# One relu and one low-part step per PSUM bank in a two-layer feed-forward network

## Chip, cores and metric

One of the eight cores of a Trainium2 chip runs the whole program. The metric is the device time of one execution in microseconds (us); it is given as the median of several runs. Beside it stands one profiled execution, from which all rows come.

## What is computed

Attention with a window of 64 over q, k and v of 8 batches, 8 heads, 576 positions and 64 features, then a Fourier mix of the 8 x 576 x 512 result, a normalisation, and a feed-forward network with two weight matrices (512 x 2048 and 2048 x 512):

```python
scores = scale * np.matmul(q, k.transpose(0, 1, 3, 2))        # masked to a window of 64
attn = softmax(scores)                                        # exp, divided by its sum
x = (attn @ v) as (B, S, H * D)
u = x + real(fft(fft(x, axis=1), axis=2))
un = (u - mean(u)) / sqrt(var(u) + 1e-6)
out = u + np.maximum(un @ w_ch1, 0.0) @ w_ch2
```

The change touches the last line alone: the relu between the two matrix products.

## The kernel before

The 4608 positions are 36 tiles of 128. Attention is done tile by tile (`attn_tile`), the Fourier mix batch by batch (`fft`), the normalisation tile by tile (`norm_tile`), and the feed-forward network for two tiles at a time: 18 chunks of 256 positions (`ffn`, names `c` and `NCH`). Each number is kept as a float16 high part and a float16 low part, and a product is three passes (`PASSES`: high-high, high-low, low-high). Chunk 0 alone is done in float32 (`plain`), while the weights are still converted and split.

In a chunk the 2048 hidden features are 16 blocks of 128, numbered by `f`. For each block:

- the first layer (`one`, L1204) is 12 matmuls of 256 columns into half a PSUM bank. A bank holds the blocks f and f + 1 for an even f, as the tile `ph`; there are two such banks (ring `f1`);
- ScalarE takes the relu of the block's 256 columns into the high part of a tile `hh` (L1219, in chunk 0 L1216);
- VectorE forms the low part, relu minus high part, from the same 256 columns (L1222);
- the second layer (`second`, L1185) is 6 matmuls of 512 columns, which add the block to the two banks `po` of the chunk (ring `f2`, two banks).

The ring `hh` has 4 tiles, so the relu of a block waits until the second layer has used the tile of four blocks earlier. At a chunk's end VectorE adds `po` to the tile `xu` (`last`, L1242, in chunk 0 L1240) and the sum is sent out.

No engine's order is written by hand. The kernel first records every operation with an engine, an estimated duration and a priority (`op`), and `Plan.order` plays them through: at each step it takes the operation that can start earliest, with the priority deciding ties and short waits. The relu and the low part have the priority -10, ahead of nearly all else on their engines; first and second layer have priorities above one million, so that PE (TensorE) does attention and Fourier work when that is ready and fills up with the feed-forward network. Some operations may be given to one of two engines (`alt`). A ring in the list of the planner's constructor hands out its buffers in a fixed order. What the planner's order leaves to wait for is made into semaphore waits afterwards, tile by tile, from what each instruction writes and reads: each engine then works its list strictly in order, and an instruction that waits holds up all behind it.

Of the kernel before, what the change touches and what calls it, by code (L numbers as in the profile page):

```python
# [12 lines left out]
F32 = mybir.dt.float32  # L13
F16 = mybir.dt.float16
# [13 lines left out]
P = 128  # L28
# [7 lines left out]
CH = 256  # L36
NCH = NTT // 2
NKF = DFF // P
XR = 10
TURN = 1.5  # L40
Y_SOON = (4, 8)
LAZY, LAZY_FFT, LAZY_U = 0.2, 0.8, 0.5
# [257 lines left out]
def attn_fft_ffn_kernel(ctx: ExitStack, tc: tile.TileContext, q, k, v, w1, w2, gidx, dft_d, dft_s, mask, out):  # L300
# [8 lines left out]

    RINGS = {  # L310
        "kq": 2, "pr": 2, "pt": 2, "xu": XR, "y": 1, "yT": 1, "tail": 1,
        "xe": 1, "r3": 3, "fh": 5, "g": 2, "mp": 2, "mt": 1, "un": 2, "up": 1, "big": 4, "hh": 4,
        "ps": 4, "f1": 2, "f2": 2,
    }
    plan = Plan(RINGS, ("kq", "pr", "pt", "xu", "y", "yT", "tail", "xe", "r3", "fh", "g", "mp", "f1", "f2", "hh"))
# [5 lines left out]
    def bank(tag, name, shape=(P, 4, P)):  # L321
        return ps.tile(list(shape), F32, tag=tag, name=name, bufs=RINGS[tag])
# [846 lines left out]
    def ffn(c):  # L1169
        plain = c < PLAIN  # L1170
        t = {}
        bpo = [Buf("f2"), Buf("f2")]
        prev = None
        at = 0 if not plain else 1

        def second(f, bh):
            def go():
                if f == 0:
                    t["po"] = [bank("f2", f"po{c}_{i}", (P, DM)) for i in range(2)]
                hh = t["hh", f]  # L1180
                for i in range(2):
                    sl = slice(P * i, P * i + P)
                    mm = [(hh[:, sl], wf[1][f])] if plain else [(hh[:, a, sl], wp[1][:, f, b_]) for a, b_ in PASSES]
                    for x, (l_, r_) in enumerate(mm):
                        nc.tensor.matmul(  # L1185
                            t["po"][i], l_, r_, start=(f == 0 and x == 0), stop=(f == NKF - 1 and x == len(mm) - 1)
                        )

            op("PE", 1.73 if plain else 1.3, 1e6 + 32 * c + 2 * max(f, 1) + 5, go, [bh, Bw[1][f + at]], bpo)

        for f in range(NKF):
            bph, bh = Buf(), Buf("hh")
            if f % 2 == 0:
                bpair, bfirst = Buf("f1"), Buf()
            g0, c0 = 4 * (f // 4), (f % 4) * P

            def one(f=f, g0=g0, c0=c0):
                ph, u = t["ph", f], uhls[c]
                if plain:
                    mm = [(wf[0][g0 + kc][:, c0 : c0 + P], u[:, kc]) for kc in range(4)]  # L1200
                else:
                    mm = [(wp[0][:, g0 + kc, a, c0 : c0 + P], u[:, b_, kc]) for kc in range(4) for a, b_ in PASSES]
                for x, (l_, r_) in enumerate(mm):
                    nc.tensor.matmul(ph, l_, r_, start=(x == 0), stop=(x == len(mm) - 1))  # L1204

            def bank1(f=f, one=one):
                if f % 2 == 0:
                    t["ph2", f] = bank("f1", f"ph{c}_{f}", (P, 2, CH))
                t["ph", f] = t["ph2", f - f % 2][:, f % 2]
                one()  # L1210

            def h_part(z, f=f):
                ph = t["ph", f]
                if plain:
                    t["hh", f] = sb([P, CH], F32, "hh", f"hh{c}_{f}")
                    nc.scalar.activation(t["hh", f], ph, AF.Relu)  # L1216
                elif z == 0:
                    t["hh", f] = sb([P, 2, CH], F16, "hh", f"hh{c}_{f}")
                    nc.scalar.activation(t["hh", f][:, 0], ph, AF.Relu)  # L1219
                else:  # L1220
                    hh = t["hh", f]
                    nc.vector.scalar_tensor_tensor(  # L1222
                        out=hh[:, 1], in0=ph, scalar=0.0, in1=hh[:, 0], op0=ALU.max, op1=ALU.subtract
                    )

            bws = [Bw[0][g0 + kc + at] for kc in range(4)]
            op("PE", 1.73 if plain else 1.31, 1e6 + 32 * c + 2 * f, bank1, [Bu[c], *bws, bfirst], [bph] if f % 2 else [bph, bfirst], holds=[bpair])
            op("ACT", 0.28, -10, lambda g=h_part: g(0), [bph], [bh], holds=[bpair])
            if not plain:
                op("DVE", 0.33, -10, lambda g=h_part: g(1), [bph], [bh], holds=[bpair], port=False)  # L1230
            if prev:
                second(*prev)
            prev = (f, bh)
        second(*prev)
        for i in range(2):
            g = 2 * c + i

            def last(i=i, g=g):
                if plain:
                    nc.vector.tensor_tensor(out=xts[g], in0=t["po"][i], in1=xts[g], op=ALU.add)  # L1240
                else:
                    nc.vector.scalar_tensor_tensor(  # L1242
                        out=xts[g], in0=t["po"][i], scalar=osc, in1=xts[g], op0=ALU.mult, op1=ALU.add
                    )

            op("DVE", 0.65, -11, last, [bpo[i]] if plain else [bpo[i], Bosc], [Bx[g]], port=False)
            op("DMA", 0.75, -11, lambda g=g: nc.sync.dma_start(of[P * g : P * g + P], xts[g]), [Bx[g]], lat=2.0)
# [67 lines left out]
```

## Time and profile before

| | |
|---|---|
| median of 3 runs | 1009.7 us (1007.56 to 1013.33) |
| the profiled execution | 1005.62 us |
| its span, first to last instruction | 1003.8 us |
| PE busy | 966.6 us (96%) |
| VectorE (DVE) busy | 669.6 us (67%) |
| ScalarE (ACT) busy | 409.4 us (41%) |
| GpSimd (POOL) busy | 279.1 us (28%) |
| granted TensorE clock, mean | 0.991 |

The profile is one execution. Times in it count from its first instruction; an engine's busy time is the sum of its instructions' bars. A matmul's bar is longer than the time after which the next one may start, so two bars in a row overlap, and a PE that is busy all the time may still be slowed. "Idle before" is the time that an engine stood still ahead of an instruction, and the name behind it is what ended that wait.

### The profile page before, as it was taken

The page shows a single profiled execution, that of the slowest core. Times are in us where ns is not written, and L with a number is a line of the kernel's source. Part 1 is how long each engine was busy: PE and PEld are TensorE (multiplying, and loading weights), DVE is VectorE, ACT ScalarE, POOL GpSimd, SP SyncE. Part 2 cuts the span into 40 slices and gives each one's busy share as a digit, 9 for nine tenths or more (in the row PEclk, how much of TensorE's full clock was granted, in tenths as well). Part 3 has the DMA queues.
Part 4 walks back from the last instruction along what each step waited for, and adds up shares of the span by engine and source line. Part 5 has one row for each costly group of instructions (what it writes and reads, how often), then busy time and mean ns, then how long its engine had stood idle before and what let it go on. Part 6 is the DMA issues. An engine that isn't in the chain of part 4 may idle for free.

```text
span 1003.8 us, 23188 instructions
## 1 busy us (share of the span) xinstructions
PE 966.6 (96%) x8984; PEld 675.8 (67%) x8984; DVE 669.6 (67%) x1983; ACT 409.4 (41%) x1030; POOL 279.1 (28%) x553
## 2 busy tenths in 40 slices
PE   7789969999999999999999999999999999999998
PEld 5576637767676667566676667666676677666664
DVE  5699998888776678675875777666867564612121
ACT  5564646663554435433452345334433232211111
POOL 0010100244366343372334344250405201400000
PEclk9899989999999999999999999999999999999999
DMA  8987663253888986775766486656634502310000
GB/s 196 229 217 216 181 182 102 72 122 76 153 177 174 177 163 133 174 143 104 182 131 147 98 164 125 150 116 150 117 97 102 96 1 67 74 32 23 1 22 21
DMA packets 309069, 123.11 MB, mean 123 GB/s; under 512 B 291096, under 2 KB 291224, under 8 KB 308960
## 3 DMA queue, kind: packets, MB, share of 16 engines
q1 hardware_dynamic: 306240, 112.72, 51.4%
q0 software_dynamic: 2720, 8.92, 3.3%
q8 instruction: 70, 1.15, 0.5%
q14 instruction: 39, 0.32, 0.1%
HBM read 54.99 MB, written 14.17 MB: 69 GB/s over the span
## 4 chain that ended last, share of the span: by engine, by line
PE 79%; DVE 8%; DMA 6%; POOL 3%; issue 2%; ACT 1%; SPq 1%; DVEq 0%; ACTq 0%; POOLq 0%
PE ph L1204 34%; PE po L1185 32%; PE pa L656 3%; PE pz L921 3%; PE pg L887 2%; DMA uhl<-up 2%; PE psc L577 2%; POOL up L413 1%; DMA qn<-in_q 1%; DMA kn<-in_k 1%; POOL flex L413 1%; PE pp L613 1%; PE psc L572 1%; PE py L747 1%; DVE pr L594 1%
## 5 line engine op out<-in xcount | busy, mean ns | idle before, releaser
L1204 PE MATMUL ph<-uhl,w0s 128*128 128x256 f16 (+1 forms) x3384 | 426.1, 276 | 6.1 <-DVE hh L1222 5.6
L1185 PE MATMUL po<-w1s,hh 128*128 128x512 f16 (+1 forms) x1696 | 425.6, 387 | 0.0
L1204 PEld LDWEIGHTS <-w0s 128*128 128x128 f16 x3264 | 316.7, 98 | 90.5 <-issue 10.2
L1219 ACT ACTIVATE hh<-ph 128x256 f16<-128x256 f32 x272 | 104.2, 383 | 397.0 <-PE ph L1204 287.9
L1222 DVE SCALAR_TENSOR_TENSOR hh<-ph,hh 128x256 f16<-128x256 f32 x272 | 114.5, 422 | 220.3 <-ACT hh L1219 204.2
L1185 PEld LDWEIGHTS <-hh 128*128 128x128 f16 x1632 | 155.5, 98 | 138.3
L602 ACT ACTIVATE pr<-pr,nm 128x128 f32<-128x128 f32 x288 | 91.1, 391 | 12.9 <-DVE nm L594 12.8
L413 POOL TENSOR_TENSOR flex<-pr,flex 128x128 f16<-128x128 f32 x112 | 53.7, 509 | 103.3 <-ACT flex L403 33.6
L413 POOL TENSOR_TENSOR up<-un,up 128x128 f16<-128x128 f32 x128 | 59.4, 493 | 59.4 <-ACT up L403 58.5
L594 DVE CUSTOM_DVE_ANT_0 pr<-psc,mskb 128x128 f32<-128x128 f32 x288 | 65.5, 284 | 14.8 <-PE psc L572 11.6
L995 POOL DMA_INDIRECT mt<-md,gix x34 | 35.9, 1056 | 90.8 <-DMA md<-mp 82.6
L413 POOL TENSOR_TENSOR flex<-qn,flex 128x128 f16<-128x128 f32 x112 | 50.9, 489 | 25.6 <-ACT flex L403 14.9
L1019 POOL TENSOR_TENSOR rs<-mv,mhalf 128x1 f32<-128x1 f32 x36 | 21.9, 607 | 125.5 <-DVE mv L1015 125.2
L413 POOL TENSOR_TENSOR flex<-kn,flex 128x128 f16<-128x128 f32 x64 | 32.1, 532 | 48.9 <-ACT flex L403 44.1
L656 PE MATMUL pa<-ve,pt 128*64 128x65 f16 (+1 forms) x760 | 43.5, 206 | 0.8 <-ACT pt L403 0.7
L656 PE MATMUL pa<-va,pt 128*64 128x65 f16 (+1 forms) x760 | 43.6, 206 | 0.0
L666 DVE TENSOR_TENSOR xu<-pa,rc 128x256 f32<-128x256 f32 x72 | 30.5, 424 | 2.8 <-DMA out<-xu 0.4
L403 ACT CAST flex<-pr 128x512 f16<-128x512 f32 x39 | 23.8, 614 | 18.2 <-DMA pt<-flex 18.0
L921 PE MATMUL pz<-g,ds__75 97*96 97x257 f16 (+3 forms) x240 | 29.1, 273 | 1.0 <-DVE g L897 0.7
L656 PEld LDWEIGHTS <-pt 128*64 128x64 f16 x1104 | 21.0, 111 | 12.8 <-issue 11.7
L613 PE MATMUL pp<-ident,pr 128*128 128x128 f32 x104 | 19.3, 300 | 10.0 <-ACT pr L602 9.5
L413 DVE TENSOR_TENSOR y<-xu 128x256 f32<-128x256 f32 x70 | 28.4, 447 | 0.7
(156 smaller groups left out, 1083.5 us busy)
## 6 DMA issues: line engine op xcount, KB each, us to landing
wd<-in_moe_w_ch SPq DMA_DIRECT2D x20, 512.0 KB, 3.4
out<-xu SPq DMA_DIRECT2D x36, 256.0 KB, 2.1
ve<-va SPq DMA_DIRECT2D x67, 130.0 KB, 3.5
kn<-in_k SPq DMA_DIRECT2D x32, 256.0 KB, 3.7
qn<-in_q SPq DMA_DIRECT2D x32, 256.0 KB, 4.3
flex<-in_moe_w_ch SPq DMA_DIRECT2D x12, 512.0 KB, 4.9
flex<-in_v SPq DMA_DIRECT2D x20, 256.0 KB
md<-mp SPq DMA_DIRECT2D x24, 192.0 KB, 2.4
```

The lines of the kernel that those rows point to most:

```text
L413: eng.tensor_tensor(out=out[:, k : k + w], in0=in0[:, k : k + w], in1=in1[:, k : k + w], op=al)
L594: nc.vector.tensor_tensor_reduce(out=t["pr", g][:, hp], in0=t["ps", g][:, hp], in1=mskb[:, m : m + P], scale=-0.125, scalar=3.0e38, op0=AL ...
L602: nc.scalar.activation(pr, pr, AF.Exp, bias=t["nm", g][:, hp : hp + 1], scale=-1.0)
L613: nc.tensor.transpose(t["pp", g][:, hp], t["pr", g][:, hp], ident)
L656: nc.tensor.matmul(pa[sl, hp], pt[:, sl], v_, start=(x == 0), stop=(x == len(mm) - 1))
L666: nc.vector.tensor_tensor(out=xv[:, g::2], in0=pa[:, :, 0:64], in1=rc.to_broadcast([P, 4, 64]), op=ALU.mult)
L921: nc.tensor.matmul(pz[:M, c0:c1], ds_[:NJ, a, c[0] : c[0] + c[1]], t["g", gi][:, b_, c0:c1], start=(x == 0), stop=(x == len(mm) - 1),)
L995: nc.gpsimd.indirect_dma_start(out=mts[T], out_offset=None, in_=mds[pb][0 : HR if n < 4 else 2 * HR], in_offset=bass.IndirectOffsetOnAxis( ...
L1185: nc.tensor.matmul(t["po"][i], l_, r_, start=(f == 0 and x == 0), stop=(f == NKF - 1 and x == len(mm) - 1))
L1204: nc.tensor.matmul(ph, l_, r_, start=(x == 0), stop=(x == len(mm) - 1))
L1219: nc.scalar.activation(t["hh", f][:, 0], ph, AF.Relu)
L1222: nc.vector.scalar_tensor_tensor(out=hh[:, 1], in0=ph, scalar=0.0, in1=hh[:, 0], op0=ALU.max, op1=ALU.subtract)
```

## The change

The relu and the low part are no longer done for each block of 256 columns but once for the two blocks of a bank, as one step of 512 columns each, into one `hh` tile of twice the size. The ring `hh` has 2 such tiles in place of 4 (the same bytes). The planner is told longer durations for the two steps (0.49 and 0.6 in place of 0.28 and 0.33), the buffer of the bank is now claimed and given back by the blocks' own operations (the helper buffers `bpair` and `bfirst` go), and the second layer's priorities are set anew, since its blocks become ready two by two. The matmuls are the same in number and shape.

```diff
+HH = 2
...
-        "xe": 1, "r3": 3, "fh": 5, "g": 2, "mp": 2, "mt": 1, "un": 2, "up": 1, "big": 4, "hh": 4,
+        "xe": 1, "r3": 3, "fh": 5, "g": 2, "mp": 2, "mt": 1, "un": 2, "up": 1, "big": 4, "hh": HH,
...
-                hh = t["hh", f]
+                hh = t["hh", f // 2]
...
-                    mm = [(hh[:, sl], wf[1][f])] if plain else [(hh[:, a, sl], wp[1][:, f, b_]) for a, b_ in PASSES]
+                    if plain:
+                        mm = [(hh[:, f % 2, sl], wf[1][f])]
+                    else:
+                        mm = [(hh[:, a, f % 2, sl], wp[1][:, f, b_]) for a, b_ in PASSES]
...
-            op("PE", 1.73 if plain else 1.3, 1e6 + 32 * c + 2 * max(f, 1) + 5, go, [bh, Bw[1][f + at]], bpo)
+            op("PE", 1.73 if plain else 1.3, 1e6 + 32 * c + 4 * max(f // 2, 1) + f % 2 + 8, go, [bh, Bw[1][f + at]], bpo)
...
-        for f in range(NKF):
-            bph, bh = Buf(), Buf("hh")
-            if f % 2 == 0:
-                bpair, bfirst = Buf("f1"), Buf()
+        for j in range(NKF // 2):
+            bph, bh = Buf("f1"), Buf("hh")
...
+                if f % 2 == 0:
+                    t["ph", f // 2] = bank("f1", f"ph{c}_{f // 2}", (P, 2, CH))
+                ph, u = t["ph", f // 2][:, f % 2], uhls[c]
...
-                    t["hh", f] = sb([P, 2, CH], F16, "hh", f"hh{c}_{f}")
-                    nc.scalar.activation(t["hh", f][:, 0], ph, AF.Relu)
+                    t["hh", j] = sb([P, 2, 2, CH], F16, "hh", f"hh{c}_{j}")
+                    nc.scalar.activation(t["hh", j][:, 0], ph, AF.Relu)
...
-            op("ACT", 0.28, -10, lambda g=h_part: g(0), [bph], [bh], holds=[bpair])
+            op("ACT", 0.49, -10, lambda g=h_part: g(0), [bph], [bh])
             if not plain:
-                op("DVE", 0.33, -10, lambda g=h_part: g(1), [bph], [bh], holds=[bpair], port=False)
+                op("DVE", 0.6, -10, lambda g=h_part: g(1), [bph], [bh], port=False)
             if prev:
-                second(*prev)
-            prev = (f, bh)
-        second(*prev)
+                for f in (0, 1):
+                    second(2 * prev[0] + f, prev[1])
+            prev = (j, bh)
+        for f in (0, 1):
+            second(2 * prev[0] + f, prev[1])
```

Since the planner sets the order, the built programs show what moved. In the rows below `ph4_8` is the bank of chunk 4 that holds the blocks 8 and 9 (before, a bank has the number of its even block; in the change `ph4_4` holds the blocks 8 and 9), `hh4_6` is the relu tile of block 6 before, and `hh4_2` that of the blocks 4 and 5 in the change; `w0s` and `w1s` are the split weights, `uhl4` the chunk's input. "waits" names the engine or DMA queue whose semaphore an instruction waits for.

PE in chunk 4, before: the end of block 8, one block of the second layer, and the start of block 9.

```order
L1204 MATMUL ph4_8_4955<-uhl4_3176,w0s_84 128x256
L1185 LDWEIGHTS hh4_6_4921 [waits Activation_49]
L1185 MATMUL po4_0_4713<-w1s_85,hh4_6_4921 128x512
...
L1185 MATMUL po4_1_4714<-w1s_85,hh4_6_4921 128x512
L1204 LDWEIGHTS w0s_84
L1204 MATMUL ph4_8_4955<-uhl4_3176,w0s_84 128x256 [waits DVE_49]
```

The same place in the change (the first-layer line is now L1208, the second-layer line L1189).

```order
L1208 MATMUL ph4_4_4827<-uhl4_3156,w0s_84 128x256
L1189 LDWEIGHTS hh4_2_4748 [waits Activation_49]
L1189 MATMUL po4_0_4640<-w1s_85,hh4_2_4748 128x512
...
L1189 MATMUL po4_1_4641<-w1s_85,hh4_2_4748 128x512
L1208 LDWEIGHTS w0s_84
L1208 MATMUL ph4_4_4827<-uhl4_3156,w0s_84 128x256
```

Before, the first matmul of block 9 waits for VectorE, and the semaphore value is that of the low part of block 8, which reads the other half of the same bank. In chunks 1 to 17 there are 136 odd blocks; 87 of them wait for the low part of their even neighbour and 12 for its relu. In the change none does.

VectorE in the same stretch of chunk 4, before (`yp`, `kn`, `py`, `flex` and `yT` belong to attention and the Fourier mix).

```order
L1222 SCALAR_TENSOR_TENSOR hh4_7_4952<-ph4_6_4889,hh4_7_4952 128x256 [waits Activation_49]
L405 TENSOR_SCALAR yp16_4978<-y16_4882 128x512 [waits DMAHW6_49,DMAHW7_49,DMAHW2_49,Pool_49]
L1222 SCALAR_TENSOR_TENSOR hh4_8_4976<-ph4_8_4955,hh4_8_4976 128x256 [waits Activation_49]
L755 SCALAR_TENSOR_TENSOR yp16_4978<-y16_4882,yp16_4978 128x512 [waits DVE_49]
L1222 SCALAR_TENSOR_TENSOR hh4_9_5004<-ph4_8_4955,hh4_9_5004 128x256 [waits Activation_49]
```

And in the change, where `hh4_4` is the step for the blocks 8 and 9.

```order
L1220 SCALAR_TENSOR_TENSOR hh4_3_4840<-ph4_3_4692,hh4_3_4840 128x512 [waits Activation_49]
L414 TENSOR_TENSOR yT3_3634<-py16_4824 128x4x128 [waits DMAHW4_49]
L414 TENSOR_TENSOR flex_78<-pr18_0_4730,flex_78 128x4x128 [waits DMAHW6_49,DMAHW5_49,Activation_49]
L1220 SCALAR_TENSOR_TENSOR hh4_4_4903<-ph4_4_4827,hh4_4_4903 128x512 [waits DVE_49,Activation_49]
L663 TENSOR_SCALAR rc17_0_4913<-pa17_0_4877 128x4 [waits PE_49]
```

The two steps of 256 columns have become one of 512, and the attention work around them has another order. Over the whole program VectorE has 136 low-part steps in place of 272 and ScalarE 144 relus in place of 288; twelve pieces of attention's low parts (`flex`: 5 of `pr`, 4 of `kn`, 3 of `qn`) have gone from POOL to VectorE. VectorE's list is the same, row by row, up to its row 438 (a weight split ahead of the first low part of chunk 1).

PE in chunk 6 of the change, where a bank is used again soonest: the second layer of block 1 ends, block 7 and the second layer of block 2 follow, and then block 8 goes into the bank that held the blocks 4 and 5.

```order
L1189 MATMUL po6_1_6243<-w1s_85,hh6_0_6118 128x512
L1208 LDWEIGHTS w0s_84
L1208 MATMUL ph6_3_6305<-uhl6_4705,w0s_84 128x256
...
L1189 LDWEIGHTS hh6_1_6239 [waits Activation_49]
L1189 MATMUL po6_0_6242<-w1s_85,hh6_1_6239 128x512
...
L1208 MATMUL ph6_4_6378<-uhl6_4705,w0s_84 128x256 [waits DVE_49]
```

The relu of the blocks 4 and 5 needs the tile `hh6_0`, which the first row of this piece is the last to read; so between that row's end and block 8 stand one block of the first layer and one of the second. Such a place, with no more than these two blocks, comes 13 times in chunks 2 to 13 of the change and 28 times in chunks 14 to 17; everywhere else (but once, in chunk 2) there is more.

## Rows read from the trace of the kernel before

**Rows 1.** The page, parts 1, 2 and 4: engines, granted clock by slices, chain.

```profile
span 1003.8 us, 23188 instructions
...
PE 966.6 (96%) x8984; PEld 675.8 (67%) x8984; DVE 669.6 (67%) x1983; ACT 409.4 (41%) x1030; POOL 279.1 (28%) x553
...
PEclk9899989999999999999999999999999999999999
...
PE 79%; DVE 8%; DMA 6%; POOL 3%; issue 2%; ACT 1%; SPq 1%; DVEq 0%; ACTq 0%; POOLq 0%
```

**Rows 2.** Windows: length, busy by engine, granted clock, DMA share, GB/s.

```profile
200.00:300.00 100.00, 99.80 (x1029) 70.70 (x1028) 82.33 (x267) 54.98 (x136) 50.65 (x104) 1.00 0.63 131
...
900.00:1003.80 103.80, 99.61 (x676) 65.84 (x673) 19.95 (x44) 14.22 (x37) 0.00 (x0) 1.00 0.04 16
```

**Rows 3.** Who PE waited for: total us, times, longest.

```profile
PE pp L613 <- ACT pr L602: 9.5, 1, 9.5
PE ph L1204 <- DVE hh L1222: 5.6, 6, 1.8
```

**Rows 4.** Windows: the longest wait of PE, and the low clock after it.

```profile
138.80:148.10 9.30, 0.00 (x0) 0.00 (x0) 9.06 (x23) 4.65 (x13) 0.00 (x0) 0.64 0.46 155
141.30:151.50 10.20, 3.27 (x28) 2.72 (x29) 9.96 (x29) 5.01 (x14) 0.00 (x0) 0.51 0.48 161
```

**Rows 5.** Timeline 347.5 to 353.2: blocks 8 and 9 of chunk 4.

```profile
348.48 1.47 PE L1204 MATMUL ph<-uhl,w0s 128*128 128x256 f16 x12
...
349.79 1.46 PE L1185 MATMUL po<-w1s,hh 128*128 128x512 f16 x6
349.99 0.38 ACT L1219 ACTIVATE hh<-ph 128x256 f16<-128x256 f32 x1 [2.22 <-PE ph L1204]
...
351.35 0.43 DVE L405 TENSOR_SCALAR yp<-y 128x512 f16<-128x512 f32 x1 [2.77 <-DMA uhl<-up]
351.69 0.42 DVE L1222 SCALAR_TENSOR_TENSOR hh<-ph,hh 128x256 f16<-128x256 f32 x1
...
352.16 1.25 PE L1204 MATMUL ph<-uhl,w0s 128*128 128x256 f16 x10 [0.91 <-DVE hh L1222]
```

**Rows 6.** Timeline 422 to 428: the longest of the six waits.

```profile
424.94 0.69 DVE L1010 TENSOR_TENSOR xu<-xu,mt 128x512 f32<-128x512 f32 x1 [2.06 <-DMA mt<-md,gix]
...
426.69 0.42 DVE L1222 SCALAR_TENSOR_TENSOR hh<-ph,hh 128x256 f16<-128x256 f32 x1
...
427.15 1.03 PE L1204 MATMUL ph<-uhl,w0s 128*128 128x256 f16 x8 [1.80 <-DVE hh L1222]
```

**Rows 7.** Timeline of PE: two of five short delays, at 268.6 and 536.5.

```profile
267.17 1.46 PE L1185 MATMUL po<-w1s,hh 128*128 128x512 f16 x6
268.71 1.03 PE L1204 MATMUL ph<-uhl,w0s 128*128 128x256 f16 x8
...
535.05 1.46 PE L1185 MATMUL po<-w1s,hh 128*128 128x512 f16 x6
...
536.60 0.60 PE L1204 MATMUL ph<-uhl,w0s 128*128 128x256 f16 x4
```

**Rows 8.** Groups by line and form: busy us, mean ns, idle before.

```profile
L1222 DVE SCALAR_TENSOR_TENSOR hh<-ph,hh 128x256 f16<-128x256 f32 x272 | 114.5, 422 | 220.3 <-ACT hh L1219 204.2 <-PE ph L1204 15.1
...
L897 DVE SCALAR_TENSOR_TENSOR g<-pg,g 97x512 f16<-97x512 f32 x24 | 16.4, 686 | 4.8 <-ACT g L403 4.7
...
L1219 ACT ACTIVATE hh<-ph 128x256 f16<-128x256 f32 x272 | 104.2, 383 | 397.0 <-PE ph L1204 287.9 <-PE po L1185 77.2 <-DVE hh L1222 28.7
...
L403 ACT ACTIVATE g<-pg 97x512 f16<-97x512 f32 x22 | 13.1, 595 | 10.9 <-PE pg L887 10.8
```

**Rows 9.** Timeline 950 to 957: a quiet stretch near the end.

```profile
950.00 1.46 PE L1185 MATMUL po<-w1s,hh 128*128 128x512 f16 x6
...
951.55 0.38 ACT L1219 ACTIVATE hh<-ph 128x256 f16<-128x256 f32 x1 [2.28 <-PE po L1185]
951.97 0.42 DVE L1222 SCALAR_TENSOR_TENSOR hh<-ph,hh 128x256 f16<-128x256 f32 x1 [2.24 <-ACT hh L1219]
```

More of the change, by code (lines that the diff above doesn't have):

```diff
@@ L1187, in go, with one @@
                         )
-            op("PE", 1.73 if plain else 1.3, 1e6 + 32 * c + 2 * max(f, 1) + 5, go, [bh, Bw[1][f + at]], bpo)
-        for f in range(NKF):
-            bph, bh = Buf(), Buf("hh")
-            if f % 2 == 0:
-                bpair, bfirst = Buf("f1"), Buf()
-            g0, c0 = 4 * (f // 4), (f % 4) * P
-            def one(f=f, g0=g0, c0=c0):
-                ph, u = t["ph", f], uhls[c]
+            op("PE", 1.73 if plain else 1.3, 1e6 + 32 * c + 4 * max(f // 2, 1) + f % 2 + 8, go, [bh, Bw[1][f + at]], bpo)
+        for j in range(NKF // 2):
+            bph, bh = Buf("f1"), Buf("hh")
+            def one(f):
+                g0, c0 = 4 * (f // 4), (f % 4) * P
+                if f % 2 == 0:
+                    t["ph", f // 2] = bank("f1", f"ph{c}_{f // 2}", (P, 2, CH))
+                ph, u = t["ph", f // 2][:, f % 2], uhls[c]
                 if plain:
@@ L1204, in one, with h_part @@
                     nc.tensor.matmul(ph, l_, r_, start=(x == 0), stop=(x == len(mm) - 1))
[L1206 to L1213, printed above, removed]
+            def h_part(z, j=j):
+                ph = t["ph", j]
                 if plain:
-                    t["hh", f] = sb([P, CH], F32, "hh", f"hh{c}_{f}")
-                    nc.scalar.activation(t["hh", f], ph, AF.Relu)
+                    t["hh", j] = sb([P, 2, CH], F32, "hh", f"hh{c}_{j}")
+                    nc.scalar.activation(t["hh", j], ph, AF.Relu)
                 elif z == 0:
-                    t["hh", f] = sb([P, 2, CH], F16, "hh", f"hh{c}_{f}")
-                    nc.scalar.activation(t["hh", f][:, 0], ph, AF.Relu)
+                    t["hh", j] = sb([P, 2, 2, CH], F16, "hh", f"hh{c}_{j}")
+                    nc.scalar.activation(t["hh", j][:, 0], ph, AF.Relu)
                 else:
-                    hh = t["hh", f]
+                    hh = t["hh", j]
                     nc.vector.scalar_tensor_tensor(
@@ L1224, in h_part @@
                     )
-            bws = [Bw[0][g0 + kc + at] for kc in range(4)]
-            op("PE", 1.73 if plain else 1.31, 1e6 + 32 * c + 2 * f, bank1, [Bu[c], *bws, bfirst], [bph] if f % 2 else [bph, bfirst], holds=[bpair])
-            op("ACT", 0.28, -10, lambda g=h_part: g(0), [bph], [bh], holds=[bpair])
+            for f in (2 * j, 2 * j + 1):
+                bws = [Bw[0][4 * (f // 4) + kc + at] for kc in range(4)]
+                op("PE", 1.73 if plain else 1.31, 1e6 + 32 * c + 2 * f, lambda f=f, one=one: one(f), [Bu[c], *bws], [bph])
+            op("ACT", 0.49, -10, lambda g=h_part: g(0), [bph], [bh])
             if not plain:
-                op("DVE", 0.33, -10, lambda g=h_part: g(1), [bph], [bh], holds=[bpair], port=False)
+                op("DVE", 0.6, -10, lambda g=h_part: g(1), [bph], [bh], port=False)
             if prev:
-                second(*prev)
-            prev = (f, bh)
-        second(*prev)
+                for f in (0, 1):
[3 more added lines that the diff above has]
+            second(2 * prev[0] + f, prev[1])
         for i in range(2):
```

## The prediction

> **What bounds the kernel now.** I read the page first: PE is busy for 96% of the span, and the chain that ended last is PE for 79% [rows 1]. Then the windows: PE is busy for 99.8% of the time from 200 to 300 us, with VectorE at 82%, and for 99.6% at the end, with VectorE at 20%, both at full clock [rows 2]. So a shorter step on VectorE or ScalarE is worth nothing by itself; it counts only where PE stands still for it. The waits of PE say where that is. One wait of 9.5 us stands alone, on a float32 attention tile [rows 3]; the windows put it at 138.8 to 148.1, with VectorE at 97% (9.06 of 9.30 us), and the clock is at 0.51, which is the lower of its two levels (1.2 of 2.4 GHz), for some 10 us from 141.3 on [rows 4]. All else that PE waits for in the feed-forward network is 5.6 us in 6 waits, each a first-layer block that waits for a low part [rows 3].
>
> The timeline shows one of the six, at 352 us [rows 5]. Block 8 ends (bar to 349.95), the second layer follows, and PE could go on with block 9 some 1.30 us after 349.79, at 351.09 (a block starts 0.16 us before the bar ahead of it ends: 348.48 + 1.47 against 349.79). It starts at 352.16, just behind the low part of block 8. That low part needed block 8 alone and its relu was done at 350.37, but it stood in VectorE's list behind a step of `yp` that waited for a DMA until 351.35. The order in the section on the change shows why PE cared: an odd block waits for the low part of its even neighbour, whose half of the bank it doesn't touch. The longest of the six, 1.8 us, is alike: VectorE stood 2.06 us for a gather ahead of the low part [rows 6].
>
> **What these waits have for margin.** From the end of the even block's bar: relu starts 0.04 later, low part 0.42 after the relu's start [rows 5, 9], lasts 0.42, and PE follows 0.05 behind (352.11 to 352.16): 0.93 us. With one second-layer block between, PE has 351.09 - 349.95 = 1.14 us. The margin is 0.2 us, at most of the 87 places where such a wait stands. Smaller delays don't show as waits, because bars overlap: at 268.71 and 536.60 a block starts 0.08 and 0.09 us after the bar ahead of it ends instead of 0.16 before, so 0.24 and 0.25 late [rows 7]. I found five such, some 1.3 us together.
>
> **The change, part by part.**
> - *The steps themselves.* VectorE: 272 at 422 ns, 114.5 us, go; 136 of 512 columns come. The nearest row is a like step from PSUM with 97 partitions, 686 ns [rows 8]: 93.3 us, 21 less. ScalarE: 272 at 383 ns, 104.2 us, against 136 at 595 ns, 80.9 us, 23 less [rows 8]. Both lie beside PE and are booked at 0. VectorE gives some of it back: at 0.69 us each (three are wider) the twelve pieces that come over from POOL cost 8 us or a little more, also hidden.
> - *The waits of odd blocks.* In the change they are gone: both halves are written before either is read. This takes away the six waits, 5.6 us, and the five short delays, 1.3 us. At least nothing of it (if PE meets the same late VectorE one block later), at most all 6.9.
> - *The waits for a free bank.* They were there before but nearly never decided. Now the tightest place is this: a pair's relu needs the `hh` tile of two pairs earlier, so it starts after the second layer's last read of it, and two PE blocks later the pair's bank is wanted. From the end of that second-layer bar: 0.09 to the relu (951.46 to 951.55) [rows 9], 0.595, 0.04, 0.686, 0.05, together 1.46 us. PE needs 1.31 + 1.30 - 0.16 = 2.45 us to get there. The margin is 1.0 us, five times that of before, and there are 13 such places in chunks 2 to 13, and one of 2.0 us in place of 2.6 between; the 28 in chunks 14 to 17 lie where VectorE's load falls towards 20% [rows 2]. A wait of s us before meant steps s + 0.2 late; here it would leave s - 0.8. Of the six (1.8 and five of 0.76 on average) that is 1.0 and next to nothing. Spread over 87 places it is far less at 14, but the steps are longer and one late pair holds two blocks: I take 0.7 us. Bounds: 0, and all 14 places at the mean of the six, 0.93 each, 13 us.
> - *The first 150 us.* VectorE's list is the same up to its row 438, so the 9.5 us wait and the low clock stay. The relus of chunk 0 now come two by two, and second-layer blocks there start later; whatever PE loses by that ahead of 138.8 is taken out of those 9.5 us of standing still [rows 3, 4]. If that cover were gone, it would cost one block of delay per pair.
> - *Attention and Fourier work.* The planner has moved it a little ahead on PE. No wait of PE for it after 200 us is in the rows, so I book 0 and leave 2 us on each side for it.
>
> Sum: -5.6 - 1.3 + 0.7 = -6.2 us. The profiled execution would go from 1005.6 to 999.4 us. It lies 4.1 us under the median of the runs, 1009.7, so the median would be 1003.5 us.
>
> **Rivals.**
> *The waits come back (no measurable change).* What made the low parts late, a VectorE list that stands behind a DMA [rows 5, 6], is not touched, and VectorE is at 82% in the fullest stretch [rows 2]. If PE loses 3 to 5 us at bank waits, at the second layer's waits for a late pair, or in a new order of attention, the sum is -1 to -4 us: 1006 to 1009. For it: the six waits were seldom among 87 places, so the gain is only as large as a few lucky orders. Against it: the margins of 1.0 us and more.
>
> *The wider step holds PE (slower).* A pair's steps take 1.46 us where a block's took 0.93, PE waits for both halves at once, and a pair that is late is late for a bank and for two second-layer blocks. Place: the 14 tight bank waits. Price: at 0.93 us each 13 us, so -6.9 + 13 = +6 us, 1016. It decides only from 12 of the 14 places on (12 x 0.93 = 11.2 us would make it about +4.3, 13 of them over 5), or if the looser places join in. Against it: it needs steps some 2 us late at nearly every place, and only 1 of 87 was that late before (1.8 us). The Trainium skill (Perfetto Trace Analysis, Optimizing Scalar/DVE Operations) has a rule that sides with this rival: where ScalarE or VectorE isn't saturated but causes bubbles on other engines, breaking instructions up may let work be done sooner. The trace agrees with its condition (VectorE at 67%, PE waits for it); by the rule this change goes the wrong way, and the time would be this rival's 1016. I weigh it low because what delayed PE in the rows was not the length of the step but a wait for a half-bank that was not needed.
>
> **How the numbers follow.** A measurement of this kernel can tell about 0.5% (5.0 us) from no change. The forecast, odd waits gone and little in their place, has 0.62; since its own spread (-3 to -8 us) lies across the bound, I count 0.50 of it as faster and 0.12 as no change. The waits that come back have 0.26, all within 0.5%. The wider step has 0.12, slower. So faster 0.50, no change 0.38, slower 0.12. The range: below, all 6.9 us regained, 2 us from attention and 2 to 3 us of spread between medians, 998; above, the waits that come back, the same 3 us, and no more than the start of the third case, 1013. The likeliest case alone is 1000 to 1007.
>
> **What would show it.** Right: no wait of a first-layer block for the low part of its own bank; the waits of PE on `hh` at 1 us or less in total instead of 5.6; low part near 0.69 us and relu near 0.60 in the groups by form, 136 of each; the 9.5 us wait and the low clock still at 139 to 151 us; the span 5 to 7 us shorter. Wrong: waits of even blocks on `hh` that add up to 4 us or more (then the second rival or the first), a wait of PE for attention that was not there before, or a first 150 us of another length, which I say nothing moves.

## The result and the profile after

Median of 5 runs each: 1009.7 us before (1007.56 to 1013.33), 1000.4 us after (999.16 to 1003.87). The ratio is 0.9909 with a 95% interval of 0.988 to 0.9937: faster, by more than the 0.5% that can be told apart, and inside the range of the prediction (1003.5, 998 to 1013). The profiled execution went from 1005.62 to 1000.41 us, its span from 1003.8 to 998.6.

The page of the change answers to [rows 1]: engines, and the groups of the three operations that the change touches.

```profile
span 998.6 us, 22725 instructions
...
PE 964.4 (97%) x8984; PEld 676.3 (68%) x8984; DVE 655.8 (66%) x1846; ACT 394.2 (39%) x893; POOL 254.3 (25%) x500
...
PEclk9899989999999999999999999999999999999999
...
L1208 PE MATMUL ph<-uhl,w0s 128*128 128x256 f16 (+1 forms) x3384 | 425.8, 277 | 0.3 <-DVE hh L1220 0.3
...
L1220 DVE SCALAR_TENSOR_TENSOR hh<-ph,hh 128x512 f16<-128x512 f32 x136 | 93.7, 689 | 156.7 <-ACT hh L1217 156.5
L1217 ACT ACTIVATE hh<-ph 128x512 f16<-128x512 f32 x136 | 81.0, 595 | 283.6 <-PE po L1189 212.1
```

The low part takes 689 ns and the relu 595, against the 686 and 595 that the prediction read from the nearest rows [rows 8]. Each has 136 instructions fewer, and the idle time of first-layer blocks on PE is 0.3 us.

The waits of PE in the change, to be read beside [rows 3] (total us, times, longest):

```profile
PE pp L614 <- ACT pr L603: 9.9, 1, 9.9
...
PE pa L657 <- DMA pt<-flex: 2.3, 2, 1.5
...
PE pa L657 <- ACT pt L404: 1.1, 2, 0.9
...
PE ph L1208 <- DVE hh L1220: 0.3, 1, 0.3
```

The 5.6 us that first-layer blocks waited for low parts are 0.3 us. The single long wait is still there. New is that attention blocks (`pa`) wait for `pt`, the float16 pieces of the softmax, where these cross a DMA queue: 2.3 us, at 353 and 432 us. Their wait for a ScalarE copy of `pt`, 1.1 us, is not new: it lies between 49 and 58 us, and the kernel before has such a wait there too:

```profile
PE pa L656 <- ACT pt L403: 0.7, 1, 0.7
```

Windows of the change (length, busy by engine, granted clock, DMA share, GB/s), which answer to [rows 2, 4]:

```profile
138.60:148.50 9.90, 0.02 (x1) 0.00 (x1) 9.66 (x24) 5.15 (x13) 0.00 (x0) 0.61 0.50 159
140.60:154.30 13.70, 5.74 (x56) 5.04 (x56) 13.36 (x40) 7.07 (x20) 0.00 (x0) 0.51 0.41 131
200.00:300.00 100.00, 100.00 (x1013) 72.19 (x1011) 81.23 (x246) 48.60 (x111) 41.63 (x91) 1.00 0.61 130
```

The long wait and the low clock are where they were. The low level lasted 13.7 us here and 10.2 in the first profile of before [rows 4]; a second and a third profile of the kernel before showed 13.7 as well, so its length is not the change's doing.

**Where the time went.** Bars on PE overlap, so waits alone do not show all that is lost. I therefore took, for every matmul from the first float16 first-layer block on, the distance from its start to the start of the next one, subtracted the usual distance after a matmul of that kind (the 40th percentile in the same profile), and summed by what comes next. The absolute sums hold the ordinary cost of changing from one kind of block to the next; what is to be read is the difference. Three profiles of before and three of the change (the first ones, and the repeats told of below):

| | ahead of `ph` | ahead of `pa` | ahead of `psc` | ahead of `po` | all | last matmul starts at |
|---|---|---|---|---|---|---|
| before | 12.2, 13.5, 12.2 | 19.8, 19.7, 19.7 | 4.2, 4.2, 4.3 | 5.6, 5.6, 5.5 | 42.9, 44.2, 42.9 | 999.1, 1000.8, 999.6 |
| the change | 4.8, 4.2, 4.3 | 22.4, 21.8, 22.4 | 4.3, 4.9, 4.8 | 5.5, 5.6, 5.6 | 37.5, 37.0, 37.5 | 993.9, 994.3, 993.9 |

In the means the first-layer blocks give back 8.2 us, attention blocks take 2.5, and all together, smaller kinds included, it is 6.0; the last matmul starts 5.8 us sooner. That is close to the sum of the prediction (-6.2), though not with the same parts.

### The profile page after: what moved, and what is told of

Same layout as the page of the kernel before. It is cut to its first block, busy times and chain, and to the rows that moved or that the text cites. A ratio compares the mean times of both kernels' runs of the same rounds, so it can differ in the third digit from the quotient of the medians.

```text
span 998.6 us, 22725 instructions
## 1 busy us (share of the span) xinstructions
PE 964.4 (97%) x8984; PEld 676.3 (68%) x8984; DVE 655.8 (66%) x1846; ACT 394.2 (39%) x893; POOL 254.3 (25%) x500
## 4 chain that ended last, share of the span: by engine, by line
PE 79%; DMA 8%; DVE 7%; POOL 2%; ACT 1%; SPq 1%; issue 1%; DVEq 0%; ACTq 0%; POOLq 0%
PE ph L1208 33%; PE po L1189 32%; PE pa L657 3%; DMA mt<-md,gix 3%; PE pz L922 3%; PE pg L888 2%; PE psc L578 2%; DMA kn<-in_k 1%; DMA pt<-flex 1%; DMA md<-mp 1%; POOL flex L414 1%; PE pp L614 1%; PE psc L573 1%; DMA qn<-in_q 1%; PE py L748 1%
## 5 line engine op out<-in xcount | busy, mean ns | idle before, releaser
L1208 PE MATMUL ph<-uhl,w0s 128*128 128x256 f16 (+1 forms) x3384 | 425.8, 277 | 0.3 <-DVE hh L1220 0.3
L1189 PE MATMUL po<-w1s,hh 128*128 128x512 f16 (+1 forms) x1696 | 426.0, 388 | 0.0
L1208 PEld LDWEIGHTS <-w0s 128*128 128x128 f16 x3264 | 316.5, 98 | 83.1 <-issue 1.9
L1189 PEld LDWEIGHTS <-hh 128*128 128x128 f16 x1632 | 155.7, 98 | 138.0
L1220 DVE SCALAR_TENSOR_TENSOR hh<-ph,hh 128x512 f16<-128x512 f32 x136 | 93.7, 689 | 156.7 <-ACT hh L1217 156.5
L1217 ACT ACTIVATE hh<-ph 128x512 f16<-128x512 f32 x136 | 81.0, 595 | 283.6 <-PE po L1189 212.1
L414 POOL TENSOR_TENSOR up<-un,up 128x128 f16<-128x128 f32 x128 | 55.4, 461 | 69.4 <-ACT up L404 69.4
L414 POOL TENSOR_TENSOR flex<-pr,flex 128x128 f16<-128x128 f32 x92 | 44.9, 516 | 96.9 <-ACT flex L404 79.3
L414 POOL TENSOR_TENSOR flex<-qn,flex 128x128 f16<-128x128 f32 x88 | 42.6, 518 | 47.4 <-ACT flex L404 34.8
L1243 DVE SCALAR_TENSOR_TENSOR xu<-po,osc,xu 128x512 f32<-128x512 f32 x34 | 23.9, 745 | 22.6 <-PE po L1189 22.6
L404 ACT CAST up<-un 128x512 f16<-128x512 f32 x34 | 21.0, 616 | 43.7 <-DMA uhl<-up 14.4
L404 ACT CAST flex<-pr 128x512 f16<-128x512 f32 x40 | 24.6, 616 | 25.4 <-DMA pt<-flex 25.3
L657 PEld LDWEIGHTS <-pt 128*64 128x64 f16 x1104 | 21.1, 111 | 16.7 <-issue 12.2
```

Source lines behind the costliest of these rows:

```text
L404: nc.scalar.mul(out, in_, scale) if scale is not None else nc.scalar.copy(out, in_)
L414: eng.tensor_tensor(out=out[:, k : k + w], in0=in0[:, k : k + w], in1=in1[:, k : k + w], op=al)
L657: nc.tensor.matmul(pa[sl, hp], pt[:, sl], v_, start=(x == 0), stop=(x == len(mm) - 1))
L1189: nc.tensor.matmul(t["po"][i], l_, r_, start=(f == 0 and x == 0), stop=(f == NKF - 1 and x == len(mm) - 1))
L1217: nc.scalar.activation(t["hh", j][:, 0], ph, AF.Relu)
L1220: nc.vector.scalar_tensor_tensor(out=hh[:, 1], in0=ph, scalar=0.0, in1=hh[:, 0], op0=ALU.max, op1=ALU.subtract)
```

## The experiments

The theory at the start: the gain is the odd blocks' wait for a half of the bank that they don't touch. The rivals: the gain lies in the width of the steps, or in the order of the work that the new priorities give. All ratios are to the kernel before, run beside each of them.

**The change with narrow steps** (`e1_split`): tile, priorities and the planner's durations of the change, so that every engine works in the change's order, but two steps of 256 columns each. Both of them come after the odd block, when the bank is whole.

```diff
-                    nc.scalar.activation(t["hh", j][:, 0], ph, AF.Relu)
+                    for i in range(2):
+                        nc.scalar.activation(t["hh", j][:, 0, i], ph[:, i], AF.Relu)
...
-                    nc.vector.scalar_tensor_tensor(
-                        out=hh[:, 1], in0=ph, scalar=0.0, in1=hh[:, 0], op0=ALU.max, op1=ALU.subtract
-                    )
+                    for i in range(2):
+                        nc.vector.scalar_tensor_tensor(
+                            out=hh[:, 1, i], in0=ph[:, i], scalar=0.0, in1=hh[:, 0, i], op0=ALU.max, op1=ALU.subtract
+                        )
```

> The change with each wide step cut in two again: two relus of 256 columns and then two low parts of 256, both after the odd block; every engine's order is as in the change. Theory (the odd block's wait was the loss): that wait stays away, so nearly all of the gain stays, 0.990 to 0.994 of before, waits of first-layer blocks on hh under 1.5 us. Rival (the gain is the smaller load, 21 us of VectorE and 23 us of ScalarE): the load is back at some 115 and 104 us, so the time goes back to 0.997 or more.

Measured: 1004.55 us against 1008.08, ratio 0.9956 (0.9938 to 0.9975). Its waits of PE hold none for `hh`. These are the long wait and those of attention, and below them, from the page and the groups by form, the engines and the narrow steps:

```profile
PE pp L614 <- ACT pr L603: 9.9, 1, 9.9
...
PE pa L657 <- DMA pt<-flex: 4.6, 3, 2.1
...
PE pa L657 <- ACT pt L404: 1.3, 2, 1.1
```

```profile
PE 966.8 (96%) x8984; PEld 677.0 (68%) x8984; DVE 667.0 (67%) x1982; ACT 402.4 (40%) x1029; POOL 253.9 (25%) x500
...
L1222 DVE SCALAR_TENSOR_TENSOR hh<-ph,hh 128x256 f16<-128x256 f32 x272 | 102.6, 419 | 156.0 <-ACT hh L1218 155.4
...
L1218 ACT ACTIVATE hh<-ph 128x256 f16<-128x256 f32 x272 | 89.2, 379 | 273.5 <-issue 123.6 <-PE po L1189 85.7 <-PE ph L1208 62.0
```

So the waits go without the wide steps, as the theory has it, but the time falls only half as far. By the count of the table above, PE loses 5.0 us ahead of first-layer blocks (12.6 before) and 24.6 ahead of attention (19.7 before, 22.2 in the change). The profiled execution, 1005.72 us, is a long one of this version, whose runs lie between 999.02 and 1006.23. Neither expectation held: the width of the steps is worth something after all.

The narrow steps put back less load than expected, 102.6 and 89.2 us in place of some 115 and 104, because bars of steps one right behind the other overlap: two low parts take 102.6 / 136 = 0.75 us together, not 2 x 0.419. With the pieces that came over from POOL, VectorE is still busy for 667.0 us, nearly the 669.6 of the kernel before, and ScalarE for 402.4 of 409.4. So the half of the gain that this version has is not a lighter load.

**The kernel before, with a planner that knows of the wait** (`e2_told`): the odd block is recorded as one that waits for its even neighbour's relu and low part. Nothing else is edited.

```diff
-                bpair, bfirst = Buf("f1"), Buf()
+                bpair, bfirst, beven = Buf("f1"), Buf(), bph
...
-            op("PE", 1.73 if plain else 1.31, 1e6 + 32 * c + 2 * f, bank1, [Bu[c], *bws, bfirst], [bph] if f % 2 else [bph, bfirst], holds=[bpair])
+            op("PE", 1.73 if plain else 1.31, 1e6 + 32 * c + 2 * f, bank1, [Bu[c], *bws, bfirst], [bph, beven] if f % 2 else [bph, bfirst], holds=[bpair])
```

> Before, but the planner is told that an odd block has to wait for its even neighbour's relu and low part, so that it can put other work between; steps of 256 columns and rings as before. Theory: 134 such waits now stand in the program, but with more work ahead of each, so the waits on hh fall from 5.6 us to 3 us or less, 0.994 to 0.998 of before. Rival (load): 1.000, waits as before. Rival (the wait as such costs, whether planned or not): more waits, so 1.000 to 1.005.

Measured: 1012.27 us, ratio 1.0034 (1.0015 to 1.0053). The waits of PE and two windows around the longest one:

```profile
PE ph L1204 <- DVE hh L1222: 9.3, 9, 3.5
```

```profile
406.00:406.60 0.60, 0.00 (x0) 0.00 (x0) 0.60 (x1) 0.60 (x3) 0.21 (x1) 1.00 1.12 201
406.60:413.40 6.80, 5.49 (x28) 2.82 (x29) 3.98 (x11) 2.62 (x6) 1.27 (x2) 0.51 1.00 213
```

The theory's expectation failed: in the new order 134 odd blocks wait for a low part in place of 87, and in this profile they lose more, 9.3 us. It is the longest of the twelve runs, 1014.77 us, so the size is not a usual one. The longest wait, 3.5 us, ends at 407.9; from 406.6 on, still within it, the granted clock is 0.51, the lower level, for 6.8 us. Ahead of it ScalarE had stood 5.15 us for a DMA of `kn` and VectorE 4.09 us for ScalarE. Such a delay is not in the planner's durations, and telling the planner of the dependency did not take the wait away.

**The kernel before with the change's priorities** (`e3_prio`), and the kernel before once more (`e4_before_again`):

```diff
-            op("PE", 1.73 if plain else 1.3, 1e6 + 32 * c + 2 * max(f, 1) + 5, go, [bh, Bw[1][f + at]], bpo)
+            op("PE", 1.73 if plain else 1.3, 1e6 + 32 * c + 4 * max(f // 2, 1) + f % 2 + 8, go, [bh, Bw[1][f + at]], bpo)
```

> Before with the change's priorities for the second layer alone; steps, rings and buffers as before. It leaves 57 of the 87 waits of odd blocks for a low part. Theory: the loss goes with the number of these waits, 57/87 of 6.9 us is left, so 2 us or so are gained, 0.996 to 0.999 of before, waits on hh 3 to 5 us. Rival (the new order made by the priorities is what gained): 0.990 to 0.993.

> The kernel before once more, for a second profile: its first profiled execution took 1005.6 us, its runs 1009.7 in the median. Theory: what makes the low parts late (DMAs that VectorE waits for) differs from one execution to the next, so in an execution of 1009 us the waits on hh are 8 us or more instead of 5.6. Rival: the 4 us more lie elsewhere (first 150 us, low clock), and the waits on hh are 5 to 6 us again.

Measured: 1008.71 us, ratio 1.0003 (0.9985 to 1.0021), and 1007.31 us for the repeat. The wait of first-layer blocks in the two profiles, in that order, and in the first that of attention for pieces that cross the queue (there is none in the second):

```profile
PE ph L1204 <- DVE hh L1222: 6.0, 7, 2.0
PE pa L656 <- DMA pt<-flex: 1.9, 3, 1.1
```

```profile
PE ph L1204 <- DVE hh L1222: 6.8, 10, 1.6
```

With the priorities alone, 57 odd blocks are left that wait for a low part (87 before), and they lose as much. The number of waits does not set the cost; the few late low parts do. These priorities alone, without the shared tile, gained nothing. (The change's whole order, with its durations and tiles, was not run without the shared tile.) The run shows one thing more: the new wait of attention is here too, 1.9 us at 415, 664 and 811 us, though the odd blocks wait as before. By the count above PE loses 2.1 us more ahead of attention than in the kernel before, nearly as much more as in the change (2.5). So that loss comes with the new order of the second layer and not from the end of the old waits.

**The change again, and one wide step at a time** (`e5_change_again`, `e6_wide_low`, `e6_wide_relu`). The second has the relu in two steps and the low part in one, the third the other way round; the edits are the two halves of the first diff above.

> The change as it stands, timed again on the chip and in the hour of the runs that stand beside it, since 0.991 and the 0.9956 of the two-step version came from different chips. Theory (the first half of the gain is the odd blocks' wait, the second half the wider steps): 0.989 to 0.993 of the kernel before, again some 4 us under the two-step version. Rival (the second half is the difference of two sessions): 0.994 to 0.997, like the two-step version. In the profile both expect under 1 us of first-layer blocks waiting for hh.

> The change with the low part one step of 512 columns, but the relu two steps of 256. ScalarE's queue has 136 steps of 383 ns more where 136 of 595 stood in for 272, +21 us busy less 0 on the path; VectorE's stays as in the change. If the second half of the gain is VectorE's lighter load (its steps of 256 columns cost 2 x 419 ns against 689), this version comes out as the change does, 0.989 to 0.993. If it is ScalarE's (2 x 379 against 595), it comes out like the two-step version, 0.994 to 0.997. If the width matters nowhere, all four of this call lie within 0.002 of each other.

> The change with the relu one step of 512 columns, but the low part two steps of 256: the mirror of the run before. If the second half of the gain is VectorE's lighter load, this one comes out like the two-step version, 0.994 to 0.997, and waits of attention blocks for pt (2.3 us for the transfer and 1.1 for ScalarE in the change, 4.6 and 1.3 in the two-step version) are long again; if it is ScalarE's, 0.989 to 0.993 with those waits as in the change. Rival: no difference, within 0.002.

Measured, against 1010.12 us for the kernel before in these runs: the change 1000.62, ratio 0.9905 (0.9891 to 0.992); wide low part only 1003.54, 0.9933 (0.9916 to 0.995); wide relu only 1003.85, 0.9941 (0.9922 to 0.9961). The change's interval ends below the one of the two-step version (0.9938 to 0.9975), and it is again 4 us under that version's median (3.3 us by the spans from first to last instruction; the two-step version's times hold more outside of these). The half versions, timed beside the change, are 2.9 and 3.2 us above it. So the second half of the gain is the width of the steps and not a difference between chips or hours.

Which of the two steps it is stays open: both half versions lie between, and their intervals overlap. Each of them alone loses most of what both together lose. Their profiles don't help: `pa` waits 3.0 + 1.0 us with the wide low part and 1.4 + 1.3 with the wide relu, so the third run's expectation of long waits was wrong, and the two profiled executions, aligned as below, end 1.0 us behind and 0.8 us ahead of the change, counted from the first float16 block on; two repeats of the change end 0.7 and 0.3 us ahead of its first profile. The wide-relu execution is nonetheless 1.9 us longer than the change's, because its first float16 block starts at 171.8 us (169.2 to 170.2 in the change), in a stretch in which the two programs do the same work. So where a half version loses its 3 us is not shown.

Where the width tells in one execution is seen when the change and the two-step version are laid side by side. Both have the same 8984 matmuls in the same order, so the start of every 200th can be compared. From 171 to 316 us the difference stays at 0.0; it rises to 1.3 by 359, stays, jumps to 4.6 between 417 and 438, and hardly moves from there on. Nearly all of it arises at three attention blocks (0.8 us at 333, 0.2 at 353 and 1.4 at 432) and in a stretch at the lower clock behind the third. This is the one near 432, first in the change and then in the two-step version (timeline: start, duration, engine, line, operation):

```profile
427.17 0.68 DVE L414 TENSOR_TENSOR flex<-pr,flex 128x512 f16<-128x512 f32 x1
...
429.30 1.23 SPq L633 DMA_TRANSPOSE pt<-flex  x1
...
430.01 1.46 PE L1189 MATMUL po<-w1s,hh 128*128 128x512 f16 x6
...
432.24 0.22 PE L657 MATMUL pa<-ve,pt 128*64 128x65 f16 x1 [0.77 <-DMA pt<-flex]
```

```profile
429.35 1.00 DVE L414 TENSOR_TENSOR flex<-pr,flex 128x512 f16<-128x512 f32 x1
...
431.60 1.46 PE L1189 MATMUL po<-w1s,hh 128*128 128x512 f16 x6
431.81 1.23 SPq L633 DMA_TRANSPOSE pt<-flex  x1
...
435.20 0.22 PE L657 MATMUL pa<-ve,pt 128*64 128x65 f16 x1 [2.15 <-DMA pt<-flex]
```

Count from the start of the second-layer block. In the change VectorE's piece of the softmax ends 2.16 us before it (430.01 - 427.85), the transposing DMA is issued 0.71 before it, and `pa` starts 2.23 behind. With narrow steps the piece ends 1.25 before it (431.60 - 430.35), the DMA is issued 0.21 behind it, and `pa` starts 3.60 behind. VectorE is 0.9 us later against PE, the DMA 0.9, and PE loses 1.4 more. Not all of that is the width: 0.32 us is the piece's own step, which took 1.00 us here and 0.68 there, and some 0.45 us is the transfer, which from its issue to the start of `pa` took 3.39 us here and 2.94 there. So at most 0.6 of the 1.4 us can come from steps further ahead in VectorE's list. Soon after, the clock fell in the two-step version:

```profile
433.00:435.20 2.20, 0.06 (x1) 0.00 (x0) 0.82 (x3) 0.56 (x2) 0.00 (x0) 1.00 0.80 202
...
436.00:439.40 3.40, 3.40 (x16) 1.89 (x15) 3.37 (x15) 1.60 (x5) 2.45 (x5) 0.56 0.40 75
```

That is 3.4 us at 0.56, which costs about another 1.5 us by this row (3.40 x 0.44). Here a pause of PE was paid twice.

**More slack ahead of attention** (`e7_slack`, `e8_before_slack`, `e8_slack13`). The planner can be told to count what an attention block of PE reads as coming later than computed: the factor `SLACK` times 1.0 us for what a DMA brings and 0.5 us for VectorE's and ScalarE's work. The edit is one number: 0.9 and 1.3 in the change, 0.9 in the kernel before.

```diff
-SLACK = 0.5
+SLACK = 0.9
```

> The change with the planner's slack ahead of an attention tile's PE blocks set to 0.9 us where it is 0.5, which puts these blocks later behind the p pieces that they read. If the 2.3 + 1.1 us of attention blocks that wait for p pieces in the change is what PE still loses in the middle of the program, they fall under 1.5 us in sum and the time is 2 to 3 us under the change's, 0.987 to 0.990. Rival: PE waits less there, but the order makes the first-layer blocks or the end later by as much: within 0.002 of the change. Third: the later blocks leave fewer first-layer blocks for the last stage's cover, and it is slower by 0.003 or more.

> The kernel before with the planner's slack ahead of attention blocks 0.9 us instead of 0.5, no other edit: 90 odd first-layer blocks still wait for the low part of their even neighbour and 10 for its relu, as before 87 and 12. Theory (the odd blocks' wait is a cost of its own, apart from late p pieces): PE still waits 5 to 8 us for hh in first-layer blocks, and since the kernel before lost only 0.1 us ahead of attention blocks there is nothing else to gain: 0.997 to 1.003. Rival (the slack is a better order for everything, the wait for hh included): under 3 us of it, 0.990 to 0.995, and the change's gain is then one of the order of the work.

> The change with that slack at 1.3 us. At 0.9 the waits for p pieces that had crossed the queues were gone and 1.0 us of waits for ScalarE's copies was left. If that was all that the slack can give, 1.3 stands within 0.0015 of 0.9 (0.987 to 0.990 of the kernel before); if the remaining 1.0 us goes as well, 0.986 to 0.988; if later attention blocks starve the last stage of first-layer work to cover with, 0.991 or more, with new waits after 950 us.

Measured: the change with 0.9 at 998.52 us, ratio 0.9888 (0.9874 to 0.9902), the fastest of the study and 2.1 us under the change in the same set of runs (the two intervals overlap a little). The kernel before with 0.9: 1009.61 against 1008.56, ratio 1.0021 (1.0004 to 1.0038). The change with 1.3: 1007.07, ratio 0.9977 (0.9959 to 0.9994). The waits of PE in these three, in that order:

```profile
PE pp L614 <- ACT pr L603: 9.6, 1, 9.6
...
PE pa L657 <- ACT pt L404: 1.0, 2, 0.7
```

```profile
PE ph L1204 <- DVE hh L1222: 6.9, 9, 1.2
...
PE ph L1204 <- DMA uhl<-up: 1.4, 1, 1.4
...
PE pa L656 <- ACT pt L403: 0.8, 1, 0.8
PE pa L656 <- DMA pt<-flex: 0.7, 1, 0.7
```

```profile
PE ph L1208 <- DVE w0s L1109: 6.6, 2, 3.6
PE ph L1208 <- DMA uhl<-up: 3.2, 1, 3.2
PE ph L1208 <- DVE wf L1109: 3.1, 1, 3.1
...
PE pa L657 <- ACT pt L404: 1.3, 2, 1.0
PE pz L922 <- DVE g L898: 0.7, 1, 0.7
...
PE ph L1208 <- DVE hh L1220: 0.6, 2, 0.3
```

In the first, the wait for pieces that cross the queue is gone from the list, and by the count above PE loses 19.5 us ahead of attention, as little as the kernel before, with 3.7 ahead of first-layer blocks; the last matmul starts at 990.6. The profiled execution, 997.06 us, is the shortest of its five. In the second the odd blocks wait as ever, and a wait of 1.4 us for `uhl` is new: the two kinds of waits are separate, and the one is not cured by the order that cures the other. The third failed in a way that none of the expectations named: with attention put off further, PE is given first-layer blocks whose weights (`w0s`, `wf`) or input (`uhl`) are not there yet, and stands 12.9 us for these. Of that, 9.7 us for weights lie between 141 and 154 us, about where the one long wait of 9.6 us stood, which is gone from its list. The 3.2 us for `uhl` are new, from 330.0 on, and behind them the clock is at 0.50 from 334.1 to 337.5. These do not add up to the 10 us by which its last matmul starts later than with 0.9; the rest stays open.

**A third profile of both** (`e9_before_third`, `e9_change_third`), for the gap between medians and profiles.

> A third profile of the kernel before. The medians fell by 9.3 and 9.5 us, the profiled executions by 5.2; two profiles of before showed 5.6 and 6.8 us of first-layer blocks waiting for hh. If the missing 3 to 4 us is that wait at its usual size, this profile, at 1008 to 1010, shows 8 us or more of it; if it lies elsewhere, the wait is 5.5 to 7 us again and the time is found in the start (ahead of the first float16 block, 171.0 and 171.4 us) or in more of the low clock (10.2 and 13.7 us).

> A third profile of the change: under 1 us of first-layer blocks waiting for hh, 2.5 to 4 us of attention blocks waiting for pt (3.4 and 3.1 before now), and 824 to 825 us from the first float16 block to the last matmul (824.9 and 824.1). Rival for the second half of the gain: if those pt waits are 5 us here, the difference to the two-step version (5.9) was chance.

Measured: 1006.07 and 1000.37 us. Before, first-layer blocks wait 5.7 us for `hh`; in the change not at all, `pa` waits 2.4 + 0.8 us for `pt`, and from the first float16 block to the last matmul it is 824.6 us. So 5.6, 6.8 and 5.7 us are the size of the old wait, and 2.3, 1.9 and 2.4 that of the new one, for the DMA. (ScalarE's part, 0.8 to 1.2 us, lies ahead of 60 us, and the three profiles of before have it with 0.7 to 1.1 us.)

## Why the prediction was right, point by point

- *The odd blocks' wait is real time.* Right. It is gone with the shared tile (0.0 to 0.6 us in eight profiles, with narrow or wide steps), it stays without it, in each of the four orders that were run (5.6 to 9.3 us in six profiles), and the version with the shared tile and narrow steps gives 0.9956. The term was 5.6 + 1.3 = 6.9 us less 0.7 for new waits; the count gives 8.2 us net, so by the count more of it was hidden in overlapping bars than the five short delays that I had found.
- *The new waits for a free bank*, 0.7 us forecast: 0.3 us in one profile, nothing in the two others. The margin of 1.0 us held, so "the wider step holds PE" had no ground. Breaking the steps up again, with both halves still behind the odd block, made the kernel slower (0.9956 against 0.9905). The rule of the Trainium skill (Perfetto Trace Analysis, Optimizing Scalar/DVE Operations) that breaking up may let work be done sooner sided with this rival. Its condition was there, VectorE at 67% with PE waiting for it, and the change, which goes the other way, is faster. The two-step version is no full trial of the rule, since neither half starts sooner in it. As the prediction had it, what PE waited for in the kernel before was the place of a low part in VectorE's list and not its length.
- *The steps themselves, booked at 0 because they lie beside PE.* This step failed. About half of the gain in the medians (0.9956 to 0.9905, some 3 to 5 us) is their width. How it reaches PE is not shown beyond one execution, where most of the difference arose at attention blocks that wait for pieces that VectorE and ScalarE prepare. A pair of narrow low parts takes 0.75 us and a wide one 0.69, a pair of narrow relus 0.66 and a wide one 0.60, so steps behind them stand only 0.06 us later at each pair; how this grows to 3 us and more is open.
- *Attention, booked at 0 with 2 us on each side.* Too small a bound: it lost 2.5 us by the count, 2.3 us of it as waits for the DMA. A wait of PE for attention that was not there before was named as a sign of being wrong, and it came. It is not the old wait in another place, since with the new priorities alone attention lost 2.1 us more while the odd blocks waited 6.0 us as ever; it comes with the new order of the second layer. The prediction had seen the new order, and booked it at 0 from the waits of the old one. With 0.9 of slack the wait is gone and 2.1 us are gained, which agrees with that.
- *The first 150 us.* Right: the long wait is 9.9 us in place of 9.5, and the low clock follows it. The first float16 block starts 1.9 us sooner in the change, with a second-layer step and some score matmuls, which stood ahead of it, now behind it.
- *The sum.* -6.2 us forecast. The three pairs of profiled executions give 1006.3 and 1000.5 in the mean (1005.62, 1007.31, 1006.07; 1000.41, 1000.77, 1000.37), -5.8. That the sum is right to 0.4 us is luck, since two errors nearly cancel: 2.0 us more at the odd blocks than forecast, and 2.5 us at attention that were not foreseen.
- *From the sum to the median.* The medians fell by 9.3 and 9.5 us, not by 6. All three profiled executions of before lie under the runs beside them (1009.7, 1008.1, 1010.6), by 4.1, 0.8 and 4.5 us; those of the change lie on its medians. To add the profile's distance to the median of before to the forecast was the wrong step, worth 3.1 us. The range held all the same, because it allowed 2 us for attention and 2 to 3 us for the medians. What the untraced runs of before lose beyond the profiled ones stays open: a third profile taken to find it was again a low one.

Not tried: giving each half of the bank a tile of its own, so that PE could write one half while VectorE reads the other. The prediction called the half-bank "not needed" by the odd block, and by the addresses that is so. By the Trainium skill (PSUM — Partial Sum Buffer, PSUM bank collisions raise a hardware error) semaphores should guard PSUM by bank and quadrant and not by address; no run here shows such a collision. By that rule the old wait could not have been left out, only made superfluous, as the change does.

## What to carry to other kernels

When two results share a PSUM bank as one tile, the second writer may have to wait for the readers of the first, as 99 of 136 odd blocks did here: look for a matmul that waits on the evacuation of a neighbour (the steps that read its half), and evacuate the bank as one. Telling the planner of the wait did not remove it here. Fewer and wider steps on engines that are only two-thirds busy, or less, still paid, some 3 to 5 us. A new order has its own waits, so read them again after each gain: here the next one, 2.3 us, yielded to one number, and too much of the same number cost more than it had brought.

## What the runs showed of the hardware

- A VectorE step of 256 columns from PSUM takes 419 ns and one of 512 takes 689; for ScalarE's relu it is 379 and 595. But two narrow steps, one right behind the other, take 754 and 656 ns together and not 838 and 758 (102.6 and 89.2 us for 136 pairs), because their bars overlap. So to break a step in two costs some 65 ns on VectorE and 61 on ScalarE.
- The lower clock level came in the middle of a busy program, with single waits of PE of 2.1, 3.2 and 3.5 us (`e1_split`, `e8_slack13`, `e2_told`), for 3.4, 3.4 and 6.8 us (granted 0.56, 0.50 and 0.51); the first two began behind the wait, the third within it. With one and the same long wait it lasted 10.2 us in one profile of the kernel before and 13.7 us in two others.
